# A Fourier-mixing and MLP kernel: the prologue's constant matrices released later, S1 evacuated over more single banks, the second batch's input issued earlier

## The chip, the cores and the metric

The kernel runs on one core of a Trainium2 chip. The metric is the device time of one execution in microseconds (us), lower being better. Times are medians of several executions. "Span" is the time from the first to the last instruction in a profile; it is some 2 us shorter than the device time.

## The reference

```python
X = np.fft.rfft(x, axis=1)                     # x: 8 x 3008 x 256
y = np.fft.irfft(X * (filt_r + 1j * filt_i), n=3008, axis=1)
h = y.reshape(24064, 256) @ w_in               # 256 x 2048
out = np.maximum(0.01 * h, h) @ w_out          # 2048 x 256
```

The kernel works in fp16 with fp32 sums. It does the transform of 3008 points as two stages, 94 x 32, each a matmul with constant matrices.

## The kernel before

For batch 0 nothing precedes the mixing, so a **prologue** does it by a path of its own: load x, stage 1 (S1, one constant matrix), evacuate PSUM into `big[0]`, transpose on VectorE, stage 2 (S2, 24 matrices `f2`), multiply by the filters, two inverse stages with transposes between. Then the main stage begins, in which TensorE does the MLP without a pause and the mixing of the next batches is woven in. The order of instructions on each engine is that of the program.

Some names: PSUM is the memory into which matmuls write, in banks; to evacuate a bank is to copy it out, and a block of one bank is called single (`pf`), of two double (`ph`). `fa_sb` and `fb_sb` are the real and the imaginary part of the filter, loaded in two halves of columns, each half in two pieces. `f2` are the matrices of S2 and `i1` those of the last inverse stage; the profile leaves numbers out of names and writes `f_sb` and `i_sb`.

The loads, as issued before:

```python
    nc.sync.dma_start(small_sb[:], small_d.ap())
    for i in (1, 0):                                   # matrices of S2, a third each
        nc.sync.dma_start(f2_sb[:, ts(i, NC // FP), :], f2_d.ap()[i])
    first_parts = ((0, 10), (10, 10), (20, 8), (28, 4))
    for n0, nn in first_parts:                         # x of batch 0, on GpSimd's queue (casts to fp16)
        x_load(0, n0, nn)
    for hf in range(2):                                # the filters, in two halves of columns
        filt_load(fa_sb, filt_r, hf * DH, DH)          # two DMAs each
        filt_load(fb_sb, filt_i, hf * DH, DH)
        if hf == 0:
            nc.gpsimd.dma_start(f2_sb[:, ts(2, NC // FP), :], f2_d.ap()[2])
    nc.gpsimd.dma_start(w_in_sb[:], ...)
```

The prologue (cut):

```python
    def upper(hf, t, copy):            # filter rows copied to the upper 64 partitions
        copy(t[64:P, :, ts(hf, DH)], t[0:64, :, ts(hf, DH)])

    def first_s2(hf, c, n, kind, on_pool=False):
        ...                            # n matmuls with f2 into a PSUM bank
        if on_pool:                    # ScalarE evacuates, GpSimd multiplies
            ...
            for i in range(2):         # 0: fa_sb, 1: fb_sb
                for j, xf in enumerate(xs):
                    nc.gpsimd.tensor_tensor(y[i][:, ts(j, 4), :], xf[:], fs[i][:, ts(j, 4), :], AL.mult)
        else:                          # VectorE multiplies out of PSUM
            for i in range(2):
                nc.vector.tensor_tensor(y[i], ps, fs[i], AL.mult)
    ...
    t1_part(0, 0, True)(), t1_part(0, 1, True)()        # two of four transposes (VectorE)
    upper(0, fa_sb, act), upper(0, fb_sb, dve)
    first_s2(0, 8, 8, "ph", True)                       # GpSimd
    t1_part(0, 2, True)()
    first_s2(0, 0, 8, "ph")                             # VectorE
    nc.vector.memset(i1_sb[:, 0, 0:2], 0.0)             # releases the load of i1
    nc.sync.dma_start(i1_sb[:], i1_d.ap())
    first_s2(0, 16, 4, "pf", True)
    for n0 in (0, N2 // 2):
        x_load(1, n0, N2 // 2)                          # x of batch 1, GpSimd's queue
    t1_part(0, 3, True)()
    first_s2(0, 20, 4, "pf")
    upper(1, fa_sb, act)
    upper(1, fb_sb, dve)
    keep_warm(4)                                        # filler matmuls
    first_s2(1, 8, 8, "ph", True)
    first_s2(1, 0, 8, "ph")
    ...                                                 # inverse stages
```

## Time and profile before

| | before |
|---|---|
| median time | 780.64 us (three runs, 779.9 to 781.18) |
| span of the profiled run | 777.8 us |
| first matmul of the main stage | 38.60 us |
| TensorE busy | 99% of the span |
| first transpose of the prologue | 15.09 us |
| second piece of the first half of fb_sb landed | 17.4 us |

A timeline line reads: start in us, length in us, engine, line of the program, operation, output <- input, shape, count (merged instructions of one kind), and in brackets the idle time ahead of it and what ended that. The line numbers of the changed kernel are four lower for most of the prologue: the copy of the filter, L313 before, is L309 there.

These are VectorE's second copy of fb_sb and GpSimd's products of that time, from the timelines of the two engines:

```profile
24.34 1.37 DVE L313 COPY fb_sb<-fb_sb 64x3072 f16<-64x3072 f16 x1
```

```profile
23.74 1.15 POOL L280 TENSOR_TENSOR prod<-fx_h_c,fa_sb 128x512 f16<-128x512 f32 x1
24.86 1.86 POOL L280 TENSOR_TENSOR prod<-fx_h_c,fb_sb 128x512 f16<-128x512 f32 x1
```

The first copy took 0.95 us with GpSimd idle. This one, of the same shape, took 1.37 and ended 0.82 us after the product that it had met. The next product took 1.86 us instead of 1.15. Two engines that share no data here made each other longer.

### The profile page before, as it was taken

What the parts mean: (1) busy time and instruction counts of PE and PEld (TensorE: products, weight loads), DVE (VectorE), ACT (ScalarE), POOL (GpSimd) and SP (SyncE); (2) the same over time, 40 slices, a digit from 0 to 9 for tenths busy, and PEclk for the clock granted to TensorE, in tenths of its full rate; (3) what the DMA queues carried; (4) which work ended last, traced back from release to release, by engine and by line L of the source; (5) the groups of instructions that cost most, each with busy time, mean ns of one, the idle gap of its engine ahead of it and who ended that gap; (6) DMA issues with size and microseconds to landing.
All of it is one profiled execution on the core that took longest, in us unless ns stands there. A gap on an engine that the chain in (4) does not pass through costs nothing.

```text
span 777.8 us, 13325 instructions
## 1 busy us (share of the span) xinstructions
PE 768.4 (99%) x5685; PEld 521.3 (67%) x5685; DVE 368.4 (47%) x464; ACT 553.7 (71%) x785; POOL 149.9 (19%) x123
## 2 busy tenths in 40 slices
PE   8899999999999999999999999999999999999998
PEld 4556666667676676666777667666667666766666
DVE  5979743764148741676407743187423765200000
ACT  4877768676787768777586775967668676666664
POOL 4955200330005200151002400025000330000000
PEclk9999999999999999999999999999999999999999
DMA  9961013110151010500105010230101000110111
GB/s 188 220 105 47 28 41 81 56 42 29 41 109 41 28 41 28 120 31 29 41 28 122 28 41 29 53 96 28 41 28 42 28 35 34 42 38 31 41 41 55
DMA packets 36282, 43.36 MB, mean 56 GB/s; under 512 B 8130, under 2 KB 34370, under 8 KB 35458
## 3 DMA queue, kind: packets, MB, share of 16 engines
q0 software_dynamic: 10048, 16.48, 12.3%
q1 hardware_dynamic: 26176, 26.04, 9.5%
q8 instruction: 44, 0.72, 0.4%
q14 instruction: 14, 0.11, 0.0%
HBM read 34.10 MB, written 24.64 MB: 76 GB/s over the span
## 4 chain that ended last, share of the span: by engine, by line
PE 95%; DVE 1%; ACT 1%; DMA 1%; issue 0%; POOL 0%; DVEq 0%; POOLq 0%
PE ph L380 41%; PE po_ps L394 41%; PE pf L175 3%; PE pf L243 2%; PE pf L215 2%; PE pf L231 2%; DMA x_sb<-in_x_dram 1%; PE pf L394 1%; PE pf L290 1%; PE ph L269 1%; ACT big L185 1%; DVE big L197 0%; DVE big L298 0%; DVE prod L283 0%; ACT big L291 0%
## 5 line engine op out<-in xcount | busy, mean ns | idle before, releaser
L385 ACT ACTIVATE gt_c<-ph 128x1024 f16<-128x1024 f32 x376 | 384.9, 1024 | 195.6 <-PE ph L380 193.7
L380 PE MATMUL ph<-yt,w_in_sb 128*128 128x512 f16 (+3 forms) x1600 | 386.5, 366 | 0.3 <-DVE yt L310 0.3
L394 PE MATMUL po_ps<-w_out_sb,gt_c 128*128 128x256 f16 x2944 | 381.5, 272 | 0.5 <-ACT ost_c_t L401 0.5
L394 PEld LDWEIGHTS <-gt_c 128*128 128x128 f16 x3008 | 290.5, 98 | 82.3 <-issue 2.4
L380 PEld LDWEIGHTS <-w_in_sb 128*128 128x128 f16 x1600 | 154.3, 98 | 97.6 <-issue 0.6
L224 POOL TENSOR_TENSOR y_b_g<-p_b_g,p_b_g 128x512 f16<-128x512 f32 x84 | 106.8, 1272 | 225.7 <-DVE p_b_g L222 225.7
L197 DVE STREAM_TRANSPOSE big<-big 128x1024 f32<-128x1024 f32 x32 | 55.9, 1843 | 126.0 <-ACT big L185 125.9
L185 ACT CAST big<-pf 128x512 f16<-128x512 f32 x186 | 106.6, 605 | 1.1 <-PE pf L256 1.1
L246 DVE CAST yt<-pf 128x376 f16<-128x376 f32 x112 | 56.3, 544 | 86.1 <-PE pf L243 86.1
L220 DVE TENSOR_TENSOR p_b_g<-pf,fa_sb 128x512 f32<-128x512 f32 x84 | 58.1, 692 | 38.4 <-PE pf L215 35.5
L401 ACT COPY ost_c_t<-po_ps 128x256 f32<-128x256 f32 x184 | 69.4, 377 | 6.6 <-PE po_ps L394 5.4
L205 DVE STREAM_TRANSPOSE big<-big 128x1024 f32<-128x1024 f32 x28 | 51.0, 1932 | 33.9 <-ACT big L185 33.9
L221 DVE TENSOR_TENSOR p_b_g<-pf,fb_sb 64x512 f32<-64x512 f32 x84 | 58.2, 692 | 1.1
L222 DVE TENSOR_TENSOR p_b_g<-pf,fb_sb 64x512 f32<-64x512 f32 x84 | 57.4, 683 | 1.1
L136 POOL DMA_DIRECT2D x_sb<-in_x_dram x13 | 7.1, 549 | 251.9 <-PE pf L175 251.1
L243 PEld LDWEIGHTS <-big 128*128 128x128 f16 x448 | 25.7, 98 | 13.2
L175 PE MATMUL pf<-x_sb,small_sb 94*128 94x512 f16 x112 | 33.6, 379 | 0.2 <-DVE yt L246 0.2
L215 PE MATMUL pf<-big,f_sb 128*128 128x256 f16 x168 | 32.1, 273 | 0.0
L231 PE MATMUL pf<-y_b_g,small_sb 128*128 128x512 f16 x84 | 31.8, 379 | 0.0
L215 PEld LDWEIGHTS <-f_sb 128*128 128x128 f16 x168 | 16.4, 98 | 19.7
L243 PE MATMUL pf<-i_sb,big 128*128 128x94 f16 x448 | 28.7, 206 | 0.0
L175 PEld LDWEIGHTS <-small_sb 94*128 94x128 f16 x112 | 10.7, 98 | 10.5
(51 smaller groups left out, 166.3 us busy)
## 6 DMA issues: line engine op xcount, KB each, us to landing
out_dram<-ost_c_t SPq DMA_DIRECT2D x92, 256.0 KB, 2.1
x_sb<-in_x_dram POOLq DMA_DIRECT2D x5, 1536.0 KB, 11.0
x_sb<-in_x_dram POOLq DMA_DIRECT2D x2, 768.0 KB, 8.2
x_sb<-in_x_dram POOLq DMA_DIRECT2D x3, 480.0 KB, 8.2
w_in_sb<-in_moe_w_in_dram POOLq DMA_DIRECT2D x1, 1024.0 KB, 13.5
w_out_sb<-in_moe_w_out_dram POOLq DMA_DIRECT2D x1, 1024.0 KB, 10.6
x_sb<-in_x_dram POOLq DMA_DIRECT2D x1, 1024.0 KB, 8.2
fa_sb<-in_filt_r_dram POOLq DMA_DIRECT2D x4, 192.0 KB, 9.6
```

Of the source, the lines that this page charges most:

```text
L175: nc.tensor.matmul(ps, fwd1[:N1], x_sb[:N1, ds(2 * g, 2), :], start=True, stop=True)
L185: copy(paired(dst)[:, ds(n0, nn), ds(e0, de)], ps.rearrange("p n (e t) -> p n e t", t=2))
L215: nc.tensor.matmul(ps[:, j, :], f2_sb[:, 2 * g + j, :], src[:, 2 * g + j, :], start=True, stop=True)
L220: nc.vector.tensor_tensor(p1[:], ps, fa, AL.mult)
L221: nc.vector.tensor_tensor(p2[0:64], ps[64:P], fb[64:P], AL.mult)
L222: nc.vector.tensor_tensor(p2[64:P], ps[0:64], fb[0:64], AL.mult)
L224: nc.gpsimd.tensor_tensor(y1[:], p1[:], p2[:], AL.add)
L243: nc.tensor.matmul(ps[:, j, :], src[:, dt, n2, :], i1_sb[:, n2, :], start=True, stop=True)
L380: nc.tensor.matmul(ph[:, j, ds(o, ln)], w_in_sb[:, dt, ts(ct, P)], yt[:, dt, ds(lo, ln)], start=(dt == 0), stop=(dt == NDT - 1),)
L385: nc.scalar.activation(gts[ci][:, ds(2 * g, 2), :], ph, AF.Lrelu)
L394: nc.tensor.matmul(po, gts[ci][:, ct, ts(tj, P)], w_out_sb[:, ct, :], start=(ct == 0), stop=(ct == NCT - 1))
L401: nc.scalar.copy(ost[:, tj % 2, :], po)
```

## The change

Three things, all in the prologue. The f2 matrices no longer go ahead of x: SyncE issues all three once VectorE has done the third evacuation of x (a small memset of f2 is the release). S1 is evacuated in eleven pieces instead of ten (one double bank becomes two single ones), with the engines given by hand, and five filler matmuls are left out. The x of batch 1 is issued on GpSimd before that engine's products, not between them.

```diff
     nc.sync.dma_start(small_sb[:], small_d.ap())
-    for i in (1, 0):
-        nc.sync.dma_start(f2_sb[:, ts(i, NC // FP), :], f2_d.ap()[i])
     ...
-        if hf == 0:
-            nc.gpsimd.dma_start(f2_sb[:, ts(2, NC // FP), :], f2_d.ap()[2])
     ...
-    keep_warm(18)
-    g = 0
-    for (n0, nn), fill in zip(first_parts, (4, 3, 1, 14)):
-        while nn:
-            n = 2 if nn % 4 or n0 >= N2 - 4 else 4
-            first_s1(n0, n, two[n // 4], (dve, act)[g % 2])
-            n0, nn, g = n0 + n, nn - n, g + 1
+    keep_warm(14)
+    n0, g = 0, 0
+    for groups, fill in (("2d 4a 4d", 4), ("2a 4d 4a", 2), ("2d 2a 4d", 1), ("2a 2a", 14)):
+        for n, by in groups.split():
+            n = int(n)
+            first_s1(n0, n, two[n // 4], act if by == "a" else dve)
+            n0, g = n0 + n, g + 1
+            if g == 3:
+                nc.vector.memset(f2_sb[:, NC // FP, 0:2], 0.0)
+                for i in (1, 0, 2):
+                    nc.sync.dma_start(f2_sb[:, ts(i, NC // FP), :], f2_d.ap()[i])
         keep_warm(fill)
+    for n0 in (0, N2 // 2):
+        x_load(1, n0, N2 // 2)
     t1_part(0, 0, True)(), t1_part(0, 1, True)()
     ...
-    for n0 in (0, N2 // 2):
-        x_load(1, n0, N2 // 2)
```

## The prediction

> **What bounds the kernel now.** I read the page first. TensorE is busy for 99% of the span, so everything after the first matmul of the mixture stage is a TensorE queue that the change does not touch:
>
> ```profile
> PE 768.4 (99%) x5685; PEld 521.3 (67%) x5685; DVE 368.4 (47%) x464; ACT 553.7 (71%) x785; POOL 149.9 (19%) x123
> ```
>
> That 99% hides a prologue: until 38.6 us (the first L380 matmul in the timeline) TensorE runs filler matmuls (L318) while it waits. Only this prologue of about 39 us can change, and what it loses or gains shifts the rest. Its path is in the chain of waits (start, length, what):
>
> ```profile
> 1.24 0.70 POOL x_sb L136
> 1.94 8.25 DMA x_sb<-in_x_dram
> ...
> 11.16 1.24 DVE big L185
> 12.39 0.04 issue
> 12.44 1.04 PE ph L256 x4
> 13.47 0.02 issue
> 13.49 1.57 ACT big L185 x2
> 15.07 0.02 issue
> 15.09 2.38 DVE big L197 x2
> ```
>
> So the chain is: x lands, S1, its evacuations (L185), the transposes (L197) at 15.09. That is what the change aims at. But the chain names one releaser per step, so I read VectorE's own timeline from there (start, length, engine, line, operation):
>
> ```profile
> 16.26 1.20 DVE L197 STREAM_TRANSPOSE big<-big 128x1024 f32<-128x1024 f32 x1
> 17.50 0.95 DVE L313 COPY fb_sb<-fb_sb 64x3072 f16<-64x3072 f16 x1
> 18.48 1.25 DVE L197 STREAM_TRANSPOSE big<-big 128x1024 f32<-128x1024 f32 x1
> 19.65 1.19 DVE L283 TENSOR_TENSOR prod<-ph,fa_sb 128x1024 f16<-128x1024 f32 x1
> ```
>
> The second line decides the case. VectorE runs in order, and between the second and third transpose it copies the filter half fb_sb to the upper partitions. The copy needs the first half of fb_sb. The DMA view, one issue at a time, gives issue time plus time to landing: its second piece was issued at 5.58 and took 11.8, so it landed at **17.4**, just as the transposes ended (17.46). The slack of the filters is therefore about zero now. From here VectorE shows no wait until 33.67, so a shift of this copy shifts the end of the prologue.
>
> The DMA view in one-microsecond stretches (queue: packets, MB, share) for 4 to 5 us, then 13 to 14 us:
>
> ```profile
> q0 software_dynamic: 32, 0.16, 84.3%
> q1 hardware_dynamic: 31, 0.06, 18.6%
> ```
>
> ```profile
> q0 software_dynamic: 719, 0.18, 182.2%
> ```
>
> First: x (q0) and the matrices f2 (q1) alternate one packet for one packet, and the matrices take bandwidth from x. Second: after x the filters, in 256-byte packets, fill the engines alone at 0.18 MB/us. By the slices, the engines stay filled from 2 to 42 us.
>
> **What the Trainium skill says.** (1) "DMA: Bandwidth & Descriptors", section "Issuing engines are not separate DMA queues": transfers issued by different engines run on the same 16 DMA engines and interleave. The trace agrees: the two lines of 4 to 5 us sum to 0.22 MB, close to what x gets alone (0.20 to 0.22 in each us from 8 to 11). Moving f2 moves its cost; it does not remove it. (2) The same page, "Queues, rings and completion order": each engine goes round its queues packet by packet, a packet holding several descriptors. The trace agrees for large rows (32 to 31). How many 256-byte filter rows go per turn no run here shows; that is my main uncertainty. (3) "TensorE: Matmul & The Clock Gate", "Part 1: The HAM clock gate": half clock after an idle window of some 3.4 us. The trace agrees in kind: the granted clock was 0.50 from 24 to 26 us after TensorE's idle near 22, and L290 matmuls there start 0.43 us apart, not 0.21.
>
> **The change, part by part.**
>
> *f2 out of x's way.* Before, matrices 1 and 0 (0.52 MB) were issued at 1.14 and 1.61 and landed at 4.2 and 8.6; the four parts of x landed at 7.54, 10.19, 12.05 and 12.84. From 3 to 8 us q0 moved 0.75 MB; alone at 0.205 per us it would have moved about 1.0, so x gains about 1.3 us (estimate from those rates). New landings: about 6.7, 9.0, 10.9, 11.6.
>
> *S1.* Fillers go from 18 to 14. The first 12 run at 0.43 us and end near 6.2, so the fillers end at about 6.65, no later than x. The last parts are cut into single banks: ScalarE 0.60, VectorE 0.69 each, against 1.02 and 1.22 for double banks. With part 4 landing at 11.6: matmuls at 12.0 (the double bank ahead of them has to be freed first), ScalarE from 12.4, two singles of 0.60, all evacuated at about 13.6. The transposes start at **13.6 instead of 15.09, a gain of 1.5 us**, and the first two end at 16.0.
>
> *The filters, though.* Now all three matrices (0.79 MB, not 0.52) come after x and in parallel with the first half of the filters. Before, matrix 2 sat behind those filters on GpSimd's queue. The third evacuation ends near 9.3 and the issue takes a microsecond to reach data, so f2 meets the queued end of x and then the filters. The engines are work-conserving: x ends at about 10.5 (landing less 1.1 us, the lag seen for all four parts), the filters' first half takes 4.4 us (0.79 MB at 0.18) and f2 2.1 us (0.79 MB at 0.37, the rate of matrix 2 in the stretch 16 to 18). Sum: 17.0, plus 1.1, so fb_sb lands at **18.1**, if f2 is through by then. That is 0.7 us later than before although x came 1.3 us earlier: 0.26 MB more goes ahead of the filters (+0.7), and f2 no longer uses the time before 3 us, when the slower software queue has not begun (about 0.2 MB, +0.5). If f2 gets only a fifth of the engines, the filters end at 10.5 + 4.4/0.8 + 1.1 = 17.1.
>
> So VectorE should do the transposes early, then stand **idle for 1 to 2 us before the copy of L313**, at 17.1 to 18.1 against 17.50: -0.4 to +0.6 us on the path.
>
> *x of the second batch ahead of the products.*
>
> ```profile
> 26.67 1.11 POOL L136 DMA_DIRECT2D x_sb<-in_x_dram x2
> 27.79 2.29 POOL L280 TENSOR_TENSOR prod<-fx_h_c,fa_sb 128x512 f16<-128x512 f32 x2
> ```
>
> This takes 1.11 us off GpSimd between products. The last product then ends near 31.2, not 32.3. But the last evacuation that uses it starts at 33.1, because ScalarE has four of 0.53 us to do from 31.51; those start after VectorE's last product. Worth about 0. The data come no earlier in a useful way either: w_in fills the queue until 28.8, x was queued by then, and its first reader is at 39.9. A small cost: i1 (issued 22.01, landed 30.3) had q1 nearly to itself from 27 to 28; with x queued it shares. I estimate landing at 31.5 to 34 against a need at 33.1. Perhaps 0 to +0.3.
>
> *Clock.* TensorE idles longer ahead of its second S2 block (from about 19 to 23.5). It is cold there already, from 23.2 to 26.65; a later restart can even save 0.1 to 0.2.
>
> Sum: copy of L313 about +0.4 (between -0.4 and +0.6, leaning to even sharing), i1 +0.1, clock -0.1, GpSimd 0: **+0.3 us, so 780.9**.
>
> **The rivals.** *A: the gain comes through.* If filters lead and f2 gets what is left, the copy follows the transposes at about 16.0 to 16.5: -1 to -1.5 us, 779.3. For it: that is the plain purpose, and evacuations did end last in the chain. Against: filters and f2 need 6.5 us of engines after x, and only 5.4 are left. *B: f2 starves.* If a turn of the software queue holds many filter rows, matrix 2 or even 0 lands after 20 us and S2 becomes the wait: +1 to +3 us. Against: f2 had its equal turn against x. *C: i1 becomes the wait* at the first inverse stage: up to +0.7.
>
> **Range and chances.** Before ran from 779.9 to 781.18, so noise alone is 0.6 either way. With rivals A and B at the ends I take 779.5 to 782.3. Two per cent is 15.6 us, 40% of the prologue: faster 0.005, slower 0.005, same 0.99.
>
> **What would show it.** Right: the first L197 starts near 13.6; VectorE idle of 1 to 2 us ahead of L313, ended by the landing of fb_sb at 17 to 18.5; the first L380 matmul within 1 us of 38.6. Wrong: L313 directly behind the transposes at 16 (A); a wait of L269 for f_sb (B); a wait of L307 for i_sb (C); fb_sb landing before 17; or a change after 45 us, which I hold to be none.

## The result

The changed kernel takes **782.88 us** (four runs, 782.67 to 783.45) against 780.48 for the kernel before in the same comparison. The ratio is 1.0032 with a 95% interval of 1.0014 to 1.0049. Ratios are the mean time of one kernel's fast runs over that of the other's of the same rounds, so they are not quite the ratio of the medians. At the 2% limit this is "same"; as a difference it is a loss of about 2.5 us, clear of noise, outside my range (779.5 to 782.3).

The profiled span is 781.0 us, 3.2 more than before's profiled run, which was one of its quicker ones (777.4 to 779.7 over all runs of before). The first matmul of the main stage starts at 41.96 us instead of 38.60, so the whole loss is in the prologue. TensorE's line on the page:

```profile
PE 767.6 (98%) x5680; PEld 521.3 (67%) x5680; DVE 370.6 (47%) x465; ACT 554.3 (71%) x786; POOL 148.9 (19%) x122
```

VectorE's timeline of the changed kernel from the first transpose, then GpSimd's:

```profile
13.42 2.37 DVE L193 STREAM_TRANSPOSE big<-big 128x1024 f32<-128x1024 f32 x2 [0.33 <-ACT big L181]
18.47 3.05 DVE L309 COPY fb_sb<-fb_sb 64x3072 f16<-64x3072 f16 x1 [2.67 <-DMA fb_sb<-in_filt_i_dram]
21.55 1.25 DVE L193 STREAM_TRANSPOSE big<-big 128x1024 f32<-128x1024 f32 x1
22.72 1.18 DVE L279 TENSOR_TENSOR prod<-ph,fa_sb 128x1024 f16<-128x1024 f32 x1
...
27.41 0.95 DVE L309 COPY fb_sb<-fb_sb 64x3072 f16<-64x3072 f16 x1
```

```profile
17.79 0.52 POOL L136 DMA_DIRECT2D x_sb<-in_x_dram  x1 [2.63 <-DMA fb_sb<-in_filt_i_dram]
18.41 2.29 POOL L276 TENSOR_TENSOR prod<-fx_h_c,fa_sb 128x512 f16<-128x512 f32 x2
21.60 2.27 POOL L276 TENSOR_TENSOR prod<-fx_h_c,fb_sb 128x512 f16<-128x512 f32 x2 [0.90 <-DVE fb_sb L309]
```

The transposes start at 13.42, as predicted, 1.67 us earlier. VectorE then waits for fb_sb, also as predicted, though for 2.67 us and not 1 to 2, and the copy starts at 18.47, 0.97 us later than before. But the copy then takes **3.05 us instead of 0.95**, and the third transpose starts at 21.55, 3.07 us later than before. That is about the whole difference in span, though not by the same terms to the end: the second copy took 0.95 us here, not 1.37, which gives 0.4 back, and the half clock and i1 (below) lose 0.4 and 0.3 again. GpSimd's two products cover the copy's first 2.2 us, and the copy ends 0.82 us after them. The first GpSimd line says why the products stand just there: GpSimd had to issue the second piece of batch 1's x ahead of them, and by the profile that issue waited for the landing of a piece of fb_sb. (Why the issue of one load waits for the landing of another, no run here tests.)

The DMA queues from 14 to 15 us (packets, MB, share of 16 engines' time):

```profile
q1 hardware_dynamic: 155, 0.28, 84.7%
q0 software_dynamic: 156, 0.04, 39.0%
```

f2 (q1) and the filters (q0) take turns and move about as many rows each: 0.28 MB are 137 rows of 2048 bytes (the other 18 packets of q1 are of 4 bytes), against 156 rows of 256. f2 is through by 17 us and the filters pay for it, with 0.04 MB per us instead of 0.18.

Near the end of the prologue, the chain of waits of the changed kernel passes through the load of i1, which VectorE releases at 25.05:

```profile
25.08 11.37 DMA i_sb<-inv_const
36.45 0.14 issue
36.59 0.68 PE pf L303 x16
```

i1 took 8.3 us to land before and 11.4 now, beside batch 1's x; TensorE waited 0.30 us for it.

Last, the granted clock. In the stretches view (engines' busy time, then the clock as third figure from the end), 24 to 26 us of before, then 26 to 28 us of the changed kernel:

```profile
24.00:26.00 2.00, 2.00 (x14) 1.37 (x12) 1.94 (x3) 1.07 (x2) 2.00 (x2) 0.50 1.05 238
```

```profile
26.00:28.00 2.00, 1.74 (x16) 1.74 (x17) 1.97 (x4) 0.58 (x2) 0.09 (x1) 0.50 1.15 236
```

Both are at half clock. In one-microsecond stretches it lasts from about 23.2 to 26.65 before and from about 22.9 to 29.7 in the changed kernel, where TensorE idles 6.65 us ahead of the second S2 block (2.01 before).

### The profile page after: what moved, and what is told of

It reads as the page before. It is cut to its first block, busy times and chain, and to the rows that moved or that the text cites. A ratio compares the mean times of both kernels' runs of the same rounds, so it can differ in the third digit from the quotient of the medians.

```text
span 781.0 us, 13319 instructions
## 1 busy us (share of the span) xinstructions
PE 767.6 (98%) x5680; PEld 521.3 (67%) x5680; DVE 370.6 (47%) x465; ACT 554.3 (71%) x786; POOL 148.9 (19%) x122
## 4 chain that ended last, share of the span: by engine, by line
PE 94%; DMA 1%; ACT 1%; issue 0%; DVE 0%
PE ph L381 41%; PE po_ps L395 41%; PE pf L171 3%; PE pf L239 2%; PE pf L211 2%; PE pf L227 2%; DMA i_sb<-inv_const 1%; PE pf L395 1%; ACT big L181 0%; PE ph L303 0%; ACT gt_c L386 0%; PE pf L303 0%; ACT ost_c_t L402 0%; DVE yt L306 0%; DVE yt L242 0%
## 5 line engine op out<-in xcount | busy, mean ns | idle before, releaser
L227 PE MATMUL pf<-y_b_g,small_sb 128*128 128x512 f16 x84 | 31.8, 379 | 0.0
```

## The experiments

**Theory P**: VectorE's fast copy and a GpSimd product exclude each other, and the changed kernel brought the copy behind a pair of products; with the copy's later start that makes the loss. **Rival D**: the copy is slow because DMA writes to the same memory are at their heaviest. **Rival C**: it is TensorE's half clock. **Rival X**: one of the other two parts of the change, the early x or the finer S1, carries the loss by itself. All experiments gave correct results. Ratios are to the kernel before, run on the same chip; in us they are the ratio less one times 780.3. Their 95% intervals are some 1.2 to 1.4 us to either side, so differences between experiments of less than that rest on the traces and not on the times.

### e1_fb_first: GpSimd waits for the copy

```diff
-            for i in range(2):
+            for i in ((1, 0) if (hf, c) == (0, 8) else (0, 1)):
```

> Changed kernel, but GpSimd's first four products take the fb_sb pair ahead of the fa_sb pair, so GpSimd waits for VectorE's copy of fb_sb and cannot run beside it. Same work, same transfers. Theory P (a GpSimd product and VectorE's fast copy exclude each other): the first copy of fb_sb takes 0.95 us, not 3.05, the third transpose starts near 19.4, not 21.55; the second copy may now meet GpSimd's products (up to +0.8 us). Time 780.8 to 781.7, 1.2 to 2.1 us under the changed kernel. Rival D (the copy is slow because the DMA engines write SBUF at the same time): the copy stays near 3 us and the time near 782.9.

Measured: 780.49 us, ratio 1.0006 (0.9991 to 1.0021), so +0.5 us where the changed kernel has +2.5. VectorE:

```profile
18.29 0.95 DVE L309 COPY fb_sb<-fb_sb 64x3072 f16<-64x3072 f16 x1 [2.68 <-DMA fb_sb<-in_filt_i_dram]
19.27 1.25 DVE L193 STREAM_TRANSPOSE big<-big 128x1024 f32<-128x1024 f32 x1
...
25.14 1.79 DVE L309 COPY fb_sb<-fb_sb 64x3072 f16<-64x3072 f16 x1
```

Same transfers, same work, another order of four products: the copy is back at 0.95 us. The copy ran at the same place among the same DMA transfers, so Rival D is out. The second copy met a product, as I had feared, and took 1.79. The time is 0.3 us better than the range I gave.

### e2_fa_twice: the suspected wait doubled

```diff
-            for i in range(2):
+            for i in ((0, 0, 1) if (hf, c) == (0, 8) else (0, 1)):
```

> Changed kernel, but GpSimd computes its first two products (fa_sb) twice in a row, same result: the suspected wait doubled. Theory P with VectorE kept out until GpSimd has a gap: the copy of fb_sb grows from 3.05 to about 5.3 us and the time to about 785.2. If VectorE is kept out for one product only, or rival D holds, the copy stays near 3.05 us and the time near 783.

Measured: 785.41 us, ratio 1.0066 (1.0051 to 1.0081). VectorE, then GpSimd:

```profile
18.33 5.26 DVE L309 COPY fb_sb<-fb_sb 64x3072 f16<-64x3072 f16 x1 [2.56 <-DMA fb_sb<-in_filt_i_dram]
```

```profile
18.28 4.49 POOL L276 TENSOR_TENSOR prod<-fx_h_c,fa_sb 128x512 f16<-128x512 f32 x4
```

Four products, 4.49 us, and the copy grew from 3.05 to 5.26. The copy, 0.05 us behind the first product, waited for all four, not for the one in progress.

### e3_f2_as_before: only the early x and the finer S1

The matrices' three issues put back as they were (the diff above, reversed, without the rest).

> Changed kernel with the three matrices f2 issued as before (1 and 0 at the start on SyncE, 2 on GpSimd's queue behind the first half of the filters); the finer S1 and the early x of the second batch stay. If the placing of f2 carries the loss: x parts land at 7.5 to 12.9 again, fb_sb lands near 17.4, its copy takes 0.95 us at about 17.5, and the time is 780.3 give or take 0.5. If the early x or the finer S1 carries it, the time stays above 782.

Measured: 780.33 us, ratio 1.0001 (0.9985 to 1.0018). The first copy started at 17.71 and took 0.95. So the late f2 is necessary for the loss, and Rival X fails: the other two parts together cost nothing that can be seen.

### e4_x1_as_before: only the late f2 and the finer S1

```diff
-    for n0 in (0, N2 // 2):
-        x_load(1, n0, N2 // 2)
     t1_part(0, 0, True)(), t1_part(0, 1, True)()
     ...
     first_s2(0, 16, 4, "pf", True)
+    for n0 in (0, N2 // 2):
+        x_load(1, n0, N2 // 2)
     t1_part(0, 3, True)()
```

> Changed kernel with the second batch's x issued where it was before; f2 and S1 as changed. fb_sb still lands near 18.4. GpSimd no longer stands waiting for fb_sb's first piece in order to issue x, so its first products start about 0.75 us earlier, at 17.7, and end near 20.0. Theory P: the copy ends near 20.8, so lasts about 2.3 us, not 3.05. i1 no longer shares with x and lands about 8.5 us after its issue, not 11.4, so the wait of L303 for it goes (-0.3). Time about 781.9. Rival D: the copy stays at 3 us, and the time near 782.6.

Measured: 781.23 us, ratio 1.0013 (0.9998 to 1.0028), +1.0 us. i1 landed 8.5 us after its issue. VectorE, then GpSimd:

```profile
18.41 1.19 DVE L309 COPY fb_sb<-fb_sb 64x3072 f16<-64x3072 f16 x1 [2.67 <-DMA fb_sb<-in_filt_i_dram]
```

```profile
17.63 2.98 POOL L276 TENSOR_TENSOR prod<-fx_h_c,fa_sb 128x512 f16<-128x512 f32 x2 [3.84 <-ACT fx_h_c L273]
```

The products started at 17.63, as expected. But the copy did not wait for both: it took its turn after the first, and the second product waited for it (2.98 us for the two, not 2.29). I had expected 2.3 us and got 1.19. So by the ratios the late f2 costs 1.0 us without the early x (both with the finer S1), the early x about 0.1 without the late f2 (e3), and both together 2.5: **the two parts interact**. The first copy's length shows it without doubt (0.95 us in e3, 1.19 in e4, 3.05 with both); the sizes in time are rough, since the intervals of e3 and e4 both include zero. The early x makes GpSimd wait for a piece of fb_sb in order to issue it, which starts the products in the same tenth of a microsecond in which the copy becomes possible.

### e12_s1_only: only the finer S1

The S1 part of the diff alone on the kernel before.

> Kernel before with the finer S1 alone (fillers 14, more single banks); all transfers issued as before. The transposes start some 0.3 us earlier, at 14.8, but the copy of fb_sb still waits for its landing at 17.4 to 17.7. So the time is that of the kernel before within 0.4 us. If the finer S1 was worth something by itself, it is over 0.4 us faster.

Measured: 780.21 us, ratio 0.9995 (0.9978 to 1.0012): no difference seen. The transposes started at 14.67 and the copy at 17.67, after 0.62 us of waiting for fb_sb. What the finer S1 saves is waited away. (The second copy met products here too and took 1.99 us.)

### e9_warm: TensorE kept busy through its long idle

```diff
-    keep_warm(4)
+    keep_warm(32)
```

> Changed kernel, but the 4 filler matmuls ahead of the second S2 block become 32, which fills TensorE's idle from 19.4 to 26.3 us. Theory C (part of the loss is TensorE's half clock after the longer idle): the granted clock stays at 1.0 through 22 to 30 us, the mean clock of a run goes from 0.995 to 0.998 or more, L286 matmuls start 0.21 us apart, and the time is 0.5 to 0.9 us under the changed kernel's. If the path runs through VectorE alone, the clock rises and the time stays within 0.3 us of the changed kernel's. The copy of fb_sb stays at 3.05 us either way.

Measured: 782.24 us, ratio 1.0027 (1.0010 to 1.0044). The granted clock was 1.000 in all four runs, against 0.993 to 0.996 for the changed kernel. The four L286 matmuls took 1.04 us, not 1.85. The spans were 780.1 to 780.7, against 780.9 to 781.6. It was run at another time. By the ratios it gained 0.4 us, by the medians 0.6; the intervals overlap, so the size is only roughly known. Rival C holds for about a fifth of the loss, not for the rest; the copy still took 3.06 us.

### e7_f2_behind: fewer bytes ahead of fb_sb

As e1, with matrix 1 at the start on SyncE and 0 and 2 behind the first half of the filters on GpSimd's queue.

```diff
     nc.sync.dma_start(small_sb[:], small_d.ap())
+    nc.sync.dma_start(f2_sb[:, ts(1, NC // FP), :], f2_d.ap()[1])
     ...
+        if hf == 0:
+            for i in (0, 2):
+                nc.gpsimd.dma_start(f2_sb[:, ts(i, NC // FP), :], f2_d.ap()[i])
     ...                                                # and no release at g == 3
```

> As e1_fb_first, but of the matrices only number 1 goes ahead (at the start on SyncE), and 0 and 2 follow the first half of the filters on GpSimd's queue: 0.52 MB fewer ahead of fb_sb. Theory B (fb_sb lands when the bytes ahead of it are through): fb_sb lands near 16.9 instead of 18.3, its copy starts there, and the third transpose at 17.9; matrix 0 lands near 17.8, in time. Time about 1.0 to 1.4 us under e1_fb_first, so 779.0 to 779.6. Rival: if matrix 0 now comes last, S2 (L265 or its line here) waits for it, the products start no earlier than in e1_fb_first, and the time stays near 780.5.

Measured: 782.03 us, ratio 1.0025 (1.0010 to 1.0040): a miss, 1.5 us slower than e1. The landing was as worked out: the first copy started at 16.83. But the second:

```profile
16.83 0.95 DVE L313 COPY fb_sb<-fb_sb 64x3072 f16<-64x3072 f16 x1 [0.53 <-DMA fb_sb<-in_filt_i_dram]
...
23.68 4.63 DVE L313 COPY fb_sb<-fb_sb 64x3072 f16<-64x3072 f16 x1
```

```profile
20.76 3.38 POOL L280 TENSOR_TENSOR prod<-fx_h_c,fa_sb 128x512 f16<-128x512 f32 x3
24.11 1.15 POOL L280 TENSOR_TENSOR prod<-fx_h_c,fb_sb 128x512 f16<-128x512 f32 x1
25.23 2.27 POOL L280 TENSOR_TENSOR prod<-fx_h_c,fa_sb 128x512 f16<-128x512 f32 x2
```

VectorE came at 23.68, in the middle of a row of products without gaps, and got in only at 27.5, when GpSimd had to wait for this very copy. The gain of 1.5 us at the first copy was more than lost at the second. The landing came as the bytes ahead of fb_sb would have it; the time was set by the conflict.

### e5, e6, e10: the transposes put into the wait

VectorE stands 2.67 us ahead of the copy, and the last two transposes (1.25 us each) need nothing that it waits for. e5 moves them ahead in the changed kernel; e6 does so in e1; e10 is e6 with batch 1's x at its old place.

```diff
+    t1_part(0, 2, True)()
+    t1_part(0, 3, True)()
     upper(0, fa_sb, act), upper(0, fb_sb, dve)
     first_s2(0, 8, 8, "ph", True)
-    t1_part(0, 2, True)()
     ...
-    t1_part(0, 3, True)()
```

> As e1_fb_first, but VectorE does all four transposes before the copy of fb_sb, in the 2.7 us in which it stands waiting for fb_sb. If that wait is on the path: transposes end near 18.2, the copy starts when fb_sb lands at 18.3 to 18.5, the products at 19.4 instead of 20.4, the second copy 2.4 us earlier; the time is 1.5 to 2.4 us under e1_fb_first, so 778.1 to 779.0. Rival: i1 or GpSimd's products become the wait (i1 landing at 32.6 against a need near 31.6): then about 779.5.

> As e6_t1_fb, but the second batch's x is issued where it was before the change. i1 lands about 8.5 us after its issue instead of 11. If i1 was the wait in e6_t1_fb, this gains 0.3 to 1.0 us on it, so 777.5 to 778.5; if GpSimd's products set the end, the 1.1 us of issuing x between them is lost again, and it is 0.5 to 1.0 us slower than e6_t1_fb.

> Changed kernel with all four transposes ahead of the copy of fb_sb and nothing else: e6_t1_fb without the new order of GpSimd's products. Theory P: the copy still starts near 18.4 to 18.6, just after GpSimd's pair of products, and takes about 3.05 us; the time is 1.5 to 2.1 us over e6_t1_fb, about 780.3 to 780.9, still 2 us under the changed kernel because the transposes no longer follow the copy. Without the port conflict it would be at 778.8.

| | us | ratio | 95% interval | first copy | second copy |
|---|---|---|---|---|---|
| e6_t1_fb | 778.83 | 0.9983 | 0.9968 to 0.9998 | 0.95 | 1.77 |
| e10_t1_fb_x1 | 779.67 | 0.9994 | 0.9979 to 1.0009 | 0.95 | 1.83 |
| e5_t1_first | 781.08 | 1.0013 | 0.9996 to 1.0030 | 3.07 | 1.77 |

VectorE in e6:

```profile
13.38 4.62 DVE L193 STREAM_TRANSPOSE big<-big 128x1024 f32<-128x1024 f32 x4 [0.35 <-ACT big L181]
18.42 0.95 DVE L309 COPY fb_sb<-fb_sb 64x3072 f16<-64x3072 f16 x1 [0.41 <-DMA fb_sb<-in_filt_i_dram]
19.40 1.23 DVE L279 TENSOR_TENSOR prod<-ph,fa_sb 128x1024 f16<-128x1024 f32 x1
```

The wait shrank from 2.67 to 0.41 us and **e6 beats both kernels**, by about 1.3 us against before (interval 0.2 to 2.5; under 2%). Its time is within what I gave. e5 has the same transposes and the conflict; the copy took the 3.07 us that I gave, the time was a little over my range. (The "port" in its expectation is the page's word, cited under "What follows".) It is 2.3 us slower than e6 by the ratios, of which TensorE's wait for i1 (1.39 us in its timeline) is a part: with the later products i1 is released later. In e10 GpSimd's products become the end: the transposes of the second half waited 1.87 us for evacuations behind them. So the early x is worth having there: about 0.9 us.

### e11_fa_ahead and e13_fa_ahead2: the second wait

In e6 VectorE waits again, 1.22 us, for the second half of fb_sb. One product with fa_sb could fill it.

```diff
             for i in range(2):
                 nc.vector.tensor_tensor(y[i], ps, fs[i], AL.mult)
+                if (hf, c, i) == (1, 0, 0):
+                    upper(1, fb_sb, dve)
```

In e11 the block of VectorE was put ahead of GpSimd's to keep the order of writes right; in e13 only GpSimd's two fb_sb products were put behind.

> As e6_t1_fb, but VectorE does one product with the second half of fa_sb ahead of the second copy of fb_sb, for which it stands waiting 1.2 us there (the first double-bank block of the second half goes ahead of GpSimd's for that). If that wait is on the path: the products end 1.2 us earlier and the time is 0.5 to 1.2 us under e6_t1_fb, so 777.6 to 778.3. Rival: GpSimd's products, which end at 31.4 us in e6_t1_fb, become the bound, or the copy falls behind a longer row of products as in e7_f2_behind: the time stays at 778.8 or rises by up to 2 us.

> The test of e11_fa_ahead without its swap of the two double-bank blocks, whose bank wait (TensorE idle 3.55 us) spoilt it: VectorE does one product with fa_sb ahead of the second copy of fb_sb, GpSimd's two fb_sb products of that half are only placed behind it in the program. The 1.2 us wait for fb_sb is filled, the products end about 1.1 us earlier than in e6_t1_fb. Time 777.6 to 778.4. If GpSimd's products (end near 31.4) bind instead: 778.4 to 778.9. If the copy falls behind GpSimd's row of products: up to 781.

Measured: e11 782.67 us, ratio 1.0026 (1.0011 to 1.0041), a miss by my own doing: with the blocks swapped, the next block's PSUM bank was the one that VectorE frees last, and TensorE stood 3.55 us:

```profile
27.55 1.04 PE L265 MATMUL ph<-big,f_sb 128*128 128x128 f16 x8 [3.55 <-DVE prod L279]
```

e13: 778.74 us, ratio 0.9983 (0.9968 to 0.9998), the same as e6. VectorE's products ended 0.74 us earlier (29.85 against 30.59), but GpSimd's at 31.8 instead of 31.4 (the first copy of e13's profiled run had started 0.4 us later, at 18.79), and the last evacuation waited for those. This was the second outcome that I had written down.

### What follows

The cause is settled by e1, e2, e3 and e4: f2 after x delays the copy of fb_sb by 1.0 us; the early x lines GpSimd's products up with that landing; the copy then loses 2.1 us to them. The page "SBUF — State Buffer" of the Trainium skill, section "Who interferes with whom", gives a reason why these two exclude each other: VectorE's copies in its fastest modes and GpSimd share a pair of ports, and whoever is first keeps it for the whole instruction. The exclusion the runs show (0.95, 3.05 and 5.26 us with none, two and four products in the way). That it is a port is the page's word; no run here shows the port itself, nor the mode in which the copy ran. VectorE's own products show no such wait: one took 1.21 us at 23.83 in the changed kernel, beside a GpSimd product of 1.16.

When VectorE gets in between two products stays open, but the kept traces hold more cases than the two sides above. In all of them the copy ended 0.81 to 0.83 us after the product that it had waited for. Where it came at most 0.06 us behind the start of the first product of a row, it waited for the whole row (the changed kernel, e2, e5 and e9: two, four, two and two products). Where it came later in a product, 0.13 to 1.04 us behind its start, it got in at that product's end in nine cases (e4's first copy, and the second copies of before, e1, e3, e5, e6, e10, e11 and e13). e7's second copy does not fit: it came 0.69 us behind a start and waited for four. e12's came 0.05 us before a product's end, and waited for the next one too.

## Why the prediction was wrong

Point by point, by its own steps.

- **S1 and the transposes: right.** The parts of x landed at 6.6, 8.9, 10.8 and 11.8 (given: 6.7, 9.0, 10.9, 11.6), the transposes started at 13.42 (given: 13.6).
- **The filters: right in mechanism, 0.3 us short.** The copy became possible at 18.4 where the sum gave 18.1. The packets answered the question that I had left open: about as many rows of f2 as of the filters, 137 against 156 in one us, so f2 was through first, and my "fifth of the engines" did not come about. One step of the sum was off without harm: f2's first row moved at 13.1, 3.9 us after its issue at 9.24, and not one; from 10 to 13 us q1 moved nothing. As f2 was still through before the filters, the same bytes lay ahead of them. VectorE's idle ahead of the copy was 2.67 us, over the 1 to 2 given.
- **"-0.4 to +0.6 us on the path": this is the step that failed.** It moves the start of the copy and keeps its length at 0.95 us. The start moved by +0.97 and the length by **+2.10**. I had checked what the copy waits for and not what runs beside it on GpSimd. e1 takes the length back and with it 2.0 us of the 2.5.
- **x of the second batch: "worth about 0": right alone, wrong in company.** e3 shows +0.1 without the late f2; with it the early x costs 1.5 us (e4 against the changed kernel). I looked at where the issues free GpSimd (26.67) and not at where they now make it wait (17.79).
- **i1: small, as said.** A wait of 0.30 us, at the top of "0 to +0.3".
- **Clock: wrong sign.** I gave -0.1 on the ground that one cold stretch stays one. The idle grew to 6.65 us and the cold stretch from about 3.4 to about 6.8; e9 puts it at +0.4 to +0.6. The trace of before also agrees less with the 3.4 us of idle in the prediction's third point than "in kind" suggests: the idle ahead of its cold stretch was 2.01 us.
- **Rivals.** A was dead for the reason given: fb_sb does land later. (The "5.4 us left" there leaves out the landing lag of 1.1 us; with it 4.4 to 4.9 are left, by the prediction's own numbers, which speaks still more against A.) B did not happen. C came true in small. None of the three was the conflict.
- **The range** was too narrow at the top because every term in it was a shift of starts; no term allowed an instruction to become longer.

That the effect is far under 2% was right.

## What to carry to other kernels

When a change moves an instruction in time, ask not only what it waits for but what it will now run beside: an instruction whose duration varies between two places of the same profile (0.95 and 1.37 us here, and its neighbour 1.15 and 1.86) may be telling that something excludes it. Moving a load out of one consumer's way put it into the next one's here; find the next consumer's slack first, and fill the wait with independent work of that engine (e6) before touching the transfers. An issue placed on a busy engine carries its own waits (17.79 us here), and these set when that engine's next work starts.

## What the Trainium skill lacked or had wrong

- "SBUF — State Buffer", section "Who interferes with whom", has the holder keep the port pair for one whole instruction, so a waiting engine would get in at its end. Here VectorE's copy waited for two products (3.05 us in all) in the changed kernel and for four (5.26 us) in e2, all of them back to back, and in e4 got in after one (1.19 us). What decides this is on no page that I found; the cases are listed under "What follows".
- "DMA: Bandwidth & Descriptors", section "Queues, rings and completion order", gives a turn as a packet of about 9 to 17 descriptors. It does not say what follows when the rows of two queues differ in size. Here both moved about as many rows, for rows of 256 bytes against 2048 (156 to 137 from 14 to 15 us) as for large rows (32 to 31 packets from 4 to 5 us in the kernel before). If the queues take turns, that is as many rows per turn on both sides; whether a turn is one row or several, such counts cannot tell. So the transfer of small rows yielded most of the engines to the one of large rows: the filters fell from 0.18 to 0.04 MB per us.
